# A windowed-attention and MLP block: one norm in halves, a copy on another engine, two transfers moved, the last inverses and copies in halves

## The chip, the cores and the metric

The kernel runs on one core of one Trainium2 chip. Times are device microseconds of one execution. A core has TensorE (PE in the profile; its weight loads are the row PEld), VectorE (DVE), ScalarE (ACT), GpSimd (POOL) and SyncE (SP), each of which runs its own instructions in order, and 16 DMA engines. Matmul results land in PSUM, eight banks of 128 x 512 fp32; everything else lives in SBUF or in DRAM.

## The reference

The input x has 2048 rows of 512. It is normalised, and the normalised rows go through an attention in which each row looks at eight earlier rows, two apart, and through a gelu block with a second norm; the first result, times the silu of the second, is added to x.

```python
def _A_ref(x, wqkv, wo):
    ...
    H = 32; Dh = D // H
    W, dil = 8, 2
    ...
    logits = jnp.einsum("bhsd,bhswd->bhsw", q, kg) * scale
    logits = jnp.where(mask[None, None, :, :], logits, -1e9)
    attn = _softmax(logits, axis=-1)
    o = jnp.einsum("bhsw,bhswd->bhsd", attn, vg)
    return (lambda x, *d: x.transpose(*d))(o, 0, 2, 1, 3).reshape(B, S, D) @ wo

def _B_ref(x, w1, w2, w3, w4):
    ...
    h = _gelu(_layernorm(x, axis=-1) @ w1)
    ...
    x1 = x + hs
    h2 = _gelu(_layernorm(x1, axis=-1) @ w3) @ w4
    return x1 + h2

x = A_x
xn = _layernorm(x, axis=-1)
s = _A_ref(xn, A_wqkv, A_wo)
g = _silu(_B_ref(xn, B_w1, B_w2, B_w3, B_w4))
return x + s * g
```

## The kernel before

Since the attention steps two rows at a time, the rows are split by parity p into two sets of 1024. Each set is two chunks of 512 rows (chunk c has p = c // 2), and a chunk is four tiles of 128 rows. The order of the instructions is written out by hand: every call below is pinned, and each engine and each DMA queue takes its instructions in the order of the program. Nearly all DMAs go through SP's queue.

**Opening.** `Norm` (line 213) holds one chunk's norm: `stats` (two VectorE instructions a tile, lines 224 and 226), `root` (line 235, two POOL instructions through `rsqrt_eps`, lines 207 and 208), `apply` (line 240, VectorE, a tile at a time, in place on `xn`). Chunk 0 is transposed on TensorE. For the other chunks `turn_dma` (line 322) issues one DMA transpose a tile on SP, into `xnT`. Lines 540 to 547 do the norm of chunk 1, with `scaled(0)` (line 293, a VectorE product that needs the row factors of chunk 0) between its statistics. `v_pair(0, 4)` and `v_pair(0, 6)` (lines 562 and 563) multiply tiles 0, 1 and then 2, 3 of chunk 1 by the v weights (line 371); `v_keep` (line 382) copies the result on ScalarE, and a DMA writes it to DRAM.

**Projections.** `proj` (line 332) writes two banks, a pair; `pair()` hands out three pairs in turn, so a projection waits until the pair three calls back has been read. `k_all` (line 358) copies each pair of k twice, times a 0/1 mask `em` of the even or the odd heads, into `kM` with stride 2: four ScalarE copies a chunk (line 363). `q_all`, `w1`, `w2` and `w3` follow the same way.

**Attention.** It runs in 18 units n, nine a parity. In unit n TensorE does the scores (line 639), the values and the sums of the weights of an earlier unit (`values`, lines 665 and 675), a share of the last MLP product (`g_w4`, line 777), and a final tile (`g_fin`, line 824). ScalarE does the exponential (line 646) and copies values (line 680), VectorE applies the mask (`band`, line 651). The sums are collected in batches of up to four units: `inverse` (line 687) takes a reciprocal on VectorE, `write_rec` (line 696) writes it to DRAM, `read_rec` (line 699) reads it back spread over the partitions, into four slots of `rr_t` (in the tile `ring`), and `apply` (line 712) multiplies the values by it. For the batches before the last full one the read comes as two halves of two slots, in two units. Batch 3 (units 12 to 15) has its inverses read in one piece at n = 17 (line 900) and applied in one piece after the loop (line 961). The last two units go through TensorE and ScalarE instead (`expand`, `keep_ps`, `apply_kept`, line 732).

**Final tiles.** `g_fin(p, i)` multiplies 128 rows of the attention by wo (four matmuls), copies the PSUM bank on ScalarE into `sg` (line 834), and does two VectorE products: times the gate in `xn` (line 838), plus x in `xo` (line 844, called `xo<-sg,xo`). The x is loaded again from DRAM by `load_xo` (line 491), two tiles a time, in the units that `xo_at` names; `stores` collects the writes of the result, two tiles each, and `flush_stores(n)` issues those that were noted in unit n or before. Each unit ends with its `load_xo` and `flush_stores(n - 2)` (lines 952 to 955). After the loop, lines 973 to 980 do tiles 1 to 6 of p = 1 whole, and tile 7 as two groups of 256 columns, each with its own copy, products and store, one on SP's queue and one on ScalarE's.

Of the kernel before, what the change touches and what calls it, by code (L numbers as in the profile page):

```python
# [8 lines left out]
AF = mybir.ActivationFunctionType  # L9
ALU = mybir.AluOpType  # L10
BF16 = mybir.dt.bfloat16
# [9 lines left out]
def kernel(  # L21
# [17 lines left out]
    PE, DVE, ACT, POOL, SP = nc.tensor, nc.vector, nc.scalar, nc.gpsimd, nc.sync  # L39

    def pin(ins):

        return tc.keep_in_program_order(ins)

    P = 128
    S = 2048
    D = 512
    F = 1376
    ND = D // P
# [4 lines left out]
    CH = 512  # L54
    NCH = S // CH
    TPC = CH // P
# [5 lines left out]
    NU = 2 * UP  # L62
# [6 lines left out]
    ov = out.flatten_outer_dims().rearrange("(m two) d -> two m d", two=2)  # L69
# [8 lines left out]
    fin = ctx.enter_context(tc.tile_pool(name="fin", bufs=8))  # L78
# [3 lines left out]
    def b8(shape, name):  # L82
        return big.tile(shape, BF16, name=name, tag="b8")
# [4 lines left out]
    PS = psp.tile([P, 8, CH], F32, name="PS")  # L88
# [12 lines left out]
    xn = [b8([P, M // P, D], f"xn{p}") for p in range(2)]  # L101
# [14 lines left out]
    for h in range(2):  # L116
        pin(SP.dma_start(
            out=wqk_sb[:, :, h * D // 2 : (h + 1) * D // 2], in_=wqkv_v[:, :, h * D // 2 : (h + 1) * D // 2]
# [31 lines left out]
    em = const.tile([P, 2], F32, name="em")  # L150
# [49 lines left out]
    kM = [kbp.tile([P, ND, MK, 2], BF16, name=f"kM{p}", tag="kM") for p in range(2)]  # L200
# [5 lines left out]
    def rsqrt_eps(dst, var):  # L206
        pin(POOL.tensor_scalar(out=dst, in0=var, scalar1=EPS, scalar2=None, op0=ALU.add))
        pin(POOL.tensor_tensor(out=dst, in0=dst, in1=nhalf[:, 0 : dst.shape[-1]], op=ALU.pow))
# [4 lines left out]
    class Norm:  # L213
# [18 lines left out]
            if half != 0:  # L232
                pin(DVE.reciprocal(out=r, in_=r))

        def root(self):
            rsqrt_eps(self.rstd, self.mv[:, :, 1])

        def apply(self, lo, hi):
            for j in range(lo, hi):
                pin(DVE.tensor_scalar(  # L240
                    out=self.dst[:, j, :], in0=self.src[:, j, :], scalar1=self.mv[:, j, 0:1],
                    scalar2=self.rstd[:, j : j + 1], op0=ALU.subtract, op1=ALU.mult,
                ))
# [46 lines left out]
    def scaled(c):  # L290
        p, k = c // 2, c % 2
        t = xn2Ts[c]
        pin(DVE.tensor_tensor(  # L293
            out=t, in0=xnT[p][:, :, k * CH : (k + 1) * CH],
            in1=t[:, ND - 1, :].unsqueeze(1).to_broadcast([P, ND, CH]), op=ALU.mult,
        ))
# [21 lines left out]
    def turn_dma(c, lo=0, hi=TPC):  # L318
        p, k = c // 2, c % 2
        for t in range(lo, hi):  # L320
            i = k * TPC + t
            pin(SP.dma_start_transpose(out=xnT[p][:, :, i * P : (i + 1) * P], in_=xn[p][:, i, :]))
# [20 lines left out]
    def chunk(t, c):  # L343
        p, k = c // 2, c % 2
        return t[p][:, :, k * CH : (k + 1) * CH]
# [9 lines left out]
        pin(POOL.memset(kM[p][:, :, 0:8, :], 0.0))  # L355
        pin(POOL.memset(kM[p][:, :, M + 8 : MK, :], 0.0))

    def k_all(c, parts=(0, 1)):
        p, k = c // 2, c % 2
        for a in parts:  # L360
            pt = proj(c, a, wqk_sb[:, :, D : 2 * D], chunk(xnT, c))
            for e in range(2):
                pin(ACT.activation(  # L363
                    kM[p][:, 2 * a : 2 * a + 2, 8 + k * CH : 8 + (k + 1) * CH, e], pt, AF.Copy, scale=em[:, e : e + 1]
                ))

    vn = {"n": 0}

# [117 lines left out]
    xo = {}  # L486
# [52 lines left out]
        q_keep(0, a, pq[a])  # L539
    l1 = Norm(x_of(1), x_of(1), TPC, "l1")  # L540
    l1.stats(0, 2)
    scaled(0)
    l1.stats(2, 4)
    l1.root()
    l1.apply(0, 4)
    turn_dma(1)
    rows2(1, l1)
    vputs = []
    k_all(0, (0,))
# [29 lines left out]
    while vputs:  # L579
# [4 lines left out]
    w1(1, 1)  # L584
    scaled(2)
    q_all(2)
    k_all(2)
    scaled(3)
    pin(SP.dma_start(
        out=w4_sb[:, 0 : NF - 1, :],  # L590
        in_=B_w4[0 : (NF - 1) * P, :].rearrange("(ft q) n -> q ft n", q=P),
# [106 lines left out]
    def read_rec(b, j=0, w=4):  # L698
        pin(SP.dma_start(
            out=rr_t[:, j : j + w].rearrange("p j a q -> p (j a q)"),  # L700
            in_=ap_of(rec_ds[b][:], [[16 * NQ, 16], [0, 8], [1, 4 * w * NQ]], 4 * j * NQ),
        ))
# [44 lines left out]
    free = [6, 7]  # L747
# [67 lines left out]
    stores = []  # L815
    now = {"n": 0}

    def g_fin(p, i, st=None, n=2, half=False, act=True, cols=None, later=None):

        c = slice(0, D) if cols is None else slice(*cols)  # L820
        W = c.stop - c.start

        def one(pt, dt):
            pin(PE.matmul(  # L824
                pt[:, 0:W], lhsT=oT[p][:, dt, i * P : (i + 1) * P], rhs=wo["sb"][:, dt, c],
                start=(dt == 0), stop=(dt == ND - 1),
            ))

        def done(pt):
            sg = fin.tile([P, D], BF16, name="sg", tag="f")[:, 0:W]  # L830
            pt = pt[:, 0:W]
            g = xn[p][:, i, c]
            if act:
                pin(ACT.activation(sg, pt, AF.Copy, scale=2.0 if half else 1.0))  # L834

            def steps():
                if act:
                    pin(DVE.tensor_tensor(out=sg, in0=sg, in1=g, op=ALU.mult))  # L838
                elif half:
                    pin(DVE.scalar_tensor_tensor(out=sg, in0=pt, scalar=2.0, in1=g, op0=ALU.mult, op1=ALU.mult))  # L840
                else:
                    pin(DVE.tensor_tensor(out=sg, in0=pt, in1=g, op=ALU.mult))
                x_o = xo[p][:, i, c]
                pin(DVE.tensor_tensor(out=x_o, in0=sg, in1=x_o, op=ALU.add))  # L844
                if cols is not None:
                    pin(st.dma_start(out=ov[p, i * P : (i + 1) * P, c], in_=x_o))
                elif st is not None:
                    stores.append((now["n"], lambda: store(st, p, i + 1 - n, n)))

            if later is None:  # L850
                steps()
            else:
                later.append(steps)

        return Group(ND, one, done)

    finals = []
    w4s = [g_w4(t, 2 if t == 15 else int(t > 12)) for t in range(16)]
# [7 lines left out]
    def flush(q):  # L866
        while q:
            q.pop(0)()

    def flush_stores(n):  # L870
        while stores and stores[0][0] <= n:
            stores.pop(0)[1]()
# [12 lines left out]
    HEAD, LAST = 6, 8  # L885
    W4 = 16 * NF - LAST - HEAD
    given = 0
    xo_at = {9: (1, 0), 12: (1, 2), 13: (1, 4), 15: (1, 6)}
    ends = {5: 0, 9: 1, 13: 2, 16: 3}
    load_va(0)  # L890
    for n in range(NU):
        now["n"] = n
        q = W4 * (n + 1) // NU - given
        given += q
        extra = small_g.get(n, [])
        if n == 0:
            w4_take(HEAD)

        if n == NU - 1:
            read_rec(3)  # L900
        for j in range(2):
            if n - 1 - j in ends and n < NU - 1:
                read_rec(ends[n - 1 - j], 2 * j, 2)
        if n == 15:
            values(13)
        scores(n)
        if 1 <= n < 16:
            band(n - 1)
        if n >= 2 and n != 15:
            values(n - 2 if n < 16 else n - 1)  # L910
        if n + 1 < NU:
            load_va(n + 1)
        if n == 4:
            load_wo()
        if n != 16:
            flush(finals)
        if n in ends:
            recs[ends[n]] = inverse()
            write_rec(ends[n])
        if n == 17:  # L920
            free += [2, 3]
            pin(ACT.preload_act_table_set("silu_and_others"))
        w4_take(q // 3)
        late = list(gates)
        gates.clear()
        flush(tanhs)
        if n == 15:
            apply(2, 0, 2)
        if n == 17:
            band(n)  # L930
        w4_take(q // 3, extra)
        if n < 15:
            flush(late)
        if 15 <= n < 17:
            band(n)
        if n == 16:
            flush(finals)
        if n == 15:
            values(14)
        w4_take(q - 2 * (q // 3), extra)  # L940
        for j in range(2):
            if n < 15 and n - 2 - j in ends:
                apply(ends[n - 2 - j], 2 * j, 2)
        if n == 16:
            apply(2, 2, 2)
        if n >= 15:
            flush(late)
            flush(gates)
        while extra:
            extra.pop(0).all()  # L950

        flush(vstores)
        if n in xo_at:
            load_xo(*xo_at[n])
        flush_stores(n - 2)

    n = NU
    now["n"] = n
    values(NU - 1)
    rec = inverse()  # L960
    apply(3)
    flush(gates)
    flush(tanhs)
    w4_take(LAST)
# [5 lines left out]
    flush(finals)  # L970
    for j in range(2):
        apply_kept(NU - 2 + j, kept[j])
    for i in range(1, 7):
        g_fin(1, i, SP if i % 2 or i == 6 else None, 1 if i == 6 else 2, half=i >= 5).all()
        if i != 6:
            flush_stores(n)
    g_fin(1, 7, SP, half=True, cols=(0, D // 2), later=finals).all()
    g_fin(1, 7, ACT, half=True, cols=(D // 2, D), later=finals).all()
    flush_stores(n)
    flush(finals)  # L980


# [28 lines left out]
```

## Time and profile before

| | |
|---|---|
| median of 3 runs | 195.97 us (195.82 to 197.27) |
| the profiled execution | 195.77 us |
| its span, first to last instruction | 194.0 us |
| mean granted TensorE clock | 0.997 |
| bytes read and written in DRAM | 17.14 MB and 6.59 MB |

The span is what the profile's rows cover; some 1.8 us of the execution lie around it. The page gives for each engine its busy time, and for each group of instructions the time its engine sat idle before it and what ended the wait. A line of the timeline reads: start, length, engine, line of the kernel, operation, output and input tiles with their shapes, number of instructions, and in brackets the idle time before the first of them with its releaser. Rows of the waits read: who waited, for whom, total time, number of waits, longest. "issue" is a wait for nothing that the profile shows. A few per cent of the matmul records can be missing.

Durations that the working uses, from the groups of instructions by form:

| work | mean or usual duration |
|---|---|
| statistics of a tile, two instructions on VectorE | 0.64 + 0.15 to 0.18 us |
| root on POOL, 128x4 | 0.23 + 1.04 us |
| apply of the norm, a tile | 0.41 us, 0.35 in a row |
| k copy on ScalarE, 128x1024 from PSUM, stride 2 | 1.40 us |
| DMA transpose, issue on SP | 1.22 us, the first 2.04 us |
| product with the inverses, 128x912 and 128x1824 | 0.62 and 1.11 us |
| copy of a final tile on ScalarE, 512 and 256 columns | 0.60 and 0.38 us |
| a final tile's two products on VectorE | 0.42 + 0.42 us |

### The profile page before, as it was taken

Reading aid. Unit: us, or ns where it says so; the run is one execution under the profiler, and the core shown is the slowest. Engines: PE = TensorE matmul, PEld = TensorE weight load, DVE = VectorE, ACT = ScalarE, POOL = GpSimd, SP = SyncE. Lnnn points to the kernel's source line nnn. Section 1 sums busy time; section 2 is a strip of 40 time slices with the busy share of each in tenths; the row PEclk is TensorE's granted clock in tenths of the full one; section 3 lists DMA queues with packets and bytes.
Section 4 is the critical chain, followed back from the end, with each engine's and each line's share of the span. In section 5 each row is a group of like instructions: output and inputs, shape, how many; then the busy total and the mean of one; then the engine's idle time right before and its main releaser. Section 6 shows DMA issues by size and latency. Waiting matters only on the chain.

```text
span 194.0 us, 5211 instructions
## 1 busy us (share of the span) xinstructions
PE 182.5 (94%) x2203; PEld 88.9 (46%) x2232; DVE 112.8 (58%) x226; ACT 132.7 (68%) x150; POOL 18.3 (9%) x58
## 2 busy tenths in 40 slices
PE   7999799999999999999999999999999999979990
PEld 2564344444444444444444444544454454544450
DVE  5896745220562996665000045565579789779694
ACT  7399838979258245165656787887778878876861
POOL 3006651000020022042000000000000000000000
PEclk9999999999999999999999999999999999999998
DMA  5999486479803113514700145356653753760724
GB/s 141 337 354 280 83 151 123 103 236 316 282 5 81 31 28 61 108 27 83 230 17 0 38 133 157 110 184 215 199 174 79 231 181 85 214 207 12 208 78 140
DMA packets 39859, 27.74 MB, mean 143 GB/s; under 512 B 18068, under 2 KB 39196, under 8 KB 39836
## 3 DMA queue, kind: packets, MB, share of 16 engines
q1 hardware_dynamic: 39692, 27.34, 50.4%
q8 instruction: 17, 0.28, 0.6%
q10 hardware_dynamic: 144, 0.07, 0.1%
q14 instruction: 6, 0.05, 0.1%
HBM read 17.14 MB, written 6.59 MB: 122 GB/s over the span
## 4 chain that ended last, share of the span: by engine, by line
PE 74%; ACT 9%; DVE 7%; DMA 5%; issue 3%; SPq 1%; ACTq 0%
PE PS L476 20%; PE PS L777 17%; PE PS L337 13%; ACT kM L363 8%; PE PS L436 5%; PE PS L808 4%; PE PS L824 3%; PE PS L665 3%; PE PS L639 3%; PE PS L371 3%; DMA ring<-rec_d 2%; DMA xn<-in_A_x_dram 2%; DVE xo L844 2%; DVE sg L838 2%; PE PS L675 2%
## 5 line engine op out<-in xcount | busy, mean ns | idle before, releaser
L476 PE MATMUL PS<-x1nT,w_sb 128*128 128x512 bf16 (+1 forms) x173 | 38.2, 379 | 0.2
L646 ACT ACTIVATE prob<-PS 128x1824 bf16<-128x1824 f32 x18 | 30.4, 1688 | 4.5 <-PE PS L639 3.7
L777 PE MATMUL PS<-w_sb,h3a 128*128 128x512 bf16 x112 | 29.3, 379 | 1.9 <-issue 1.7
L482 ACT ACTIVATE h3a<-PS 128x1024 bf16<-128x1024 f32 x16 | 16.4, 1024 | 20.6 <-PE PS L476 19.4
L790 DVE TENSOR_TENSOR xn<-PS,xn 128x512 bf16<-128x512 f32 x15 | 10.3, 685 | 31.8 <-PE PS L777 31.5
L476 PEld LDWEIGHTS <-w_sb 128*128 128x128 bf16 (+1 forms) x176 | 17.6, 100 | 20.4
L337 PE MATMUL PS<-xnT,wqk_sb 128*128 128x512 bf16 x110 | 24.9, 379 | 0.2
L363 ACT ACTIVATE kM<-PS,em 128x1024 bf16<-128x1024 f32 x16 | 20.8, 1401 | 2.2 <-PE PS L337 2.1
L651 DVE TENSOR_TENSOR prob<-prob,maskb 128x1824 bf16<-128x1824 bf16 x18 | 19.8, 1102 | 1.3 <-ACT prob L646 1.3
L777 PEld LDWEIGHTS <-h3a 128*128 128x128 bf16 x128 | 11.3, 97 | 13.4 <-issue 1.2
L444 DVE TENSOR_TENSOR xn<-PS,xn 128x1024 bf16<-128x1024 f32 x8 | 9.6, 1213 | 13.4 <-PE PS L436 13.4
L337 PEld LDWEIGHTS <-wqk_sb 128*128 128x128 bf16 x112 | 10.9, 97 | 13.3 <-issue 0.3
L824 PE MATMUL PS<-wo_sb,oT 128*128 128x512 bf16 (+1 forms) x68 | 15.6, 366 | 0.1
L834 ACT ACTIVATE sg<-PS 128x512 bf16<-128x512 f32 (+1 forms) x17 | 9.6, 572 | 7.4 <-PE PS L824 7.2
L337 PE MATMUL PS<-xn2T,w_sb 128*128 128x512 bf16 x62 | 14.4, 379 | 0.3 <-ACT kM L363 0.3
L436 PE MATMUL PS<-w_sb,hT 128*128 128x512 bf16 x63 | 14.4, 379 | 0.1
L382 ACT ACTIVATE vst<-PS 128x512 bf16<-128x512 f32 (+1 forms) x12 | 8.8, 736 | 7.5 <-DMA v_d<-vst 3.5
L777 PE MATMUL PS<-w_sb,h3b 128*128 128x512 bf16 (+1 forms) x44 | 12.8, 380 | 0.8 <-issue 0.8
L293 DVE TENSOR_TENSOR xn2T<-xnT,xn2T 128x2048 bf16<-128x2048 bf16 x4 | 4.9, 1217 | 11.8 <-DMA xn2T<-r_d 8.7
L409 ACT ACTIVATE hT<-PS 128x1024 bf16<-128x1024 f32 x8 | 7.9, 1038 | 4.3 <-PE PS L337 4.3
L224 DVE BATCH_NORM_STATS2 l1s<-xn 128x6 f32<-128x512 bf16 x16 | 10.1, 680 | 1.0 <-DMA xn<-in_A_x_dram 0.9
L224 DVE BATCH_NORM_STATS2 l3s<-xn 128x6 f32<-128x512 bf16 x16 | 10.3, 683 | 0.2
(104 smaller groups left out, 220.0 us busy)
## 6 DMA issues: line engine op xcount, KB each, us to landing
ring<-v_d SPq DMA_DIRECT2D x18, 256.0 KB, 2.7
v_d<-vst SPq DMA_DIRECT2D x16, 256.0 KB, 3.3
xo<-in_A_x_dram SPq DMA_DIRECT2D x8, 256.0 KB, 4.7
out_dram<-xo SPq DMA_DIRECT2D x7, 256.0 KB, 2.1
xn<-in_A_x_dram SPq DMA_DIRECT2D x6, 256.0 KB, 4.5
w_sb<-in_B_w_dram SPq DMA_DIRECT2D x1, 1376.0 KB
ring<-rec_d SPq DMA_DIRECT2D x6, 228.0 KB
w_sb<-in_B_w_dram SPq DMA_DIRECT2D x1, 1280.0 KB
```

The source lines that it names most:

```text
L224: pin(DVE.bn_stats(out=self.st[:, j, :], in_=self.src[:, j, :]))
L337: pin(PE.matmul(pt[:, b, :], lhsT=w[:, dt, nt * P : (nt + 1) * P], rhs=rhs[:, dt, :], start=(dt == 0), stop=(dt == ND - 1),))
L363: pin(ACT.activation(kM[p][:, 2 * a : 2 * a + 2, 8 + k * CH : 8 + (k + 1) * CH, e], pt, AF.Copy, scale=em[:, e : e + 1]))
L436: pin(PE.matmul(pt[:, j, :], lhsT=w2_src(p, g, m0), rhs=w2_sb[:, g, :], start=(g == 0), stop=(g == ND - 1),))
L444: pin(DVE.tensor_tensor(out=xs, in0=pts[h], in1=xs, op=ALU.add))
L476: pin(PE.matmul(pt[:fs, ft % 2, :], lhsT=w3_sb[:, dt, ft * P : ft * P + fs], rhs=x1nT[:, dt, :], start=(dt == 0), stop=(dt == ND - 1),))
L482: pin(ACT.activation(t[:, o : o + 2, :], pt, AF.Gelu_apprx_tanh))
L646: pin(ACT.activation(pr, S_ps[:, :, 0 : ND * NQ], AF.Exp, scale=SCALE))
L651: pin(DVE.tensor_tensor(out=f, in0=f, in1=maskb[:], op=ALU.min))
L777: pin(PE.matmul(pt, lhsT=h3_of(c, ft)[:fs, jj * P : (jj + 1) * P], rhs=w4_sb[:fs, ft, :], start=(ft == 0), stop=(ft == NF - 1 and silu < 2),))
L790: pin(DVE.tensor_tensor(out=x_i, in0=pt, in1=x_i, op=ALU.add))
L824: pin(PE.matmul(pt[:, 0:W], lhsT=oT[p][:, dt, i * P : (i + 1) * P], rhs=wo["sb"][:, dt, c], start=(dt == 0), stop=(dt == ND - 1),))
```

## The change

1. The norm of chunk 1: the root is taken for tiles 0 and 1 right after their statistics, and the two are applied and sent to their transposes before the statistics of tile 3; tiles 2 and 3 follow with a root of their own. `root` takes a range.
2. `k_all(2)` is called in two parts, with `scaled(3)` between them; in the second part the copy for the odd heads is done by VectorE from the same PSUM pair.
3. The last load of x, (1, 6), moves from the end of unit 15 to the end of unit 16, and unit 15 issues no stores; unit 16 issues what unit 15 would have.
4. The inverses of batch 3 are read in two DMAs of two slots each, both at n = 17, and applied in two products after the loop.
5. `g_fin` loses its arguments for columns and for work without ScalarE. With `parts=2` its matmuls run over the columns in two halves, the second half in another bank of the free list, with a ScalarE copy for each half into one tile `sg`; the two VectorE products and the store are whole. After the loop tiles 4 to 7 run so, tiles 1 to 3 as before; tile 7 has one store, on SP's queue.

```diff
-        def root(self):
-            rsqrt_eps(self.rstd, self.mv[:, :, 1])
+        def root(self, lo=0, hi=TPC):
+            rsqrt_eps(self.rstd[:, lo:hi], self.mv[:, lo:hi, 1])
...
-    def k_all(c, parts=(0, 1)):
+    def k_all(c, parts=(0, 1), both=True):
...
             for e in range(2):
...
+                dst = kM[p][:, 2 * a : 2 * a + 2, 8 + k * CH : 8 + (k + 1) * CH, e]
+                if e == 0 or both:
+                    pin(ACT.activation(dst, pt, AF.Copy, scale=em[:, e : e + 1]))
+                else:
+                    pin(DVE.tensor_scalar(out=dst, in0=pt, scalar1=em[:, e : e + 1], scalar2=None, op0=ALU.mult))
...
     l1.stats(0, 2)
+    l1.root(0, 2)
     scaled(0)
-    l1.stats(2, 4)
-    l1.root()
-    l1.apply(0, 4)
-    turn_dma(1)
+    l1.stats(2, 3)
+    l1.apply(0, 2)
+    turn_dma(1, 0, 2)
+    l1.stats(3, 4)
+    l1.root(2, 4)
+    l1.apply(2, 4)
+    turn_dma(1, 2, 4)
     rows2(1, l1)
...
-    k_all(2)
+    k_all(2, (0,))
     scaled(3)
+    k_all(2, (1,), both=False)
...
+    def g_fin(p, i, st=None, n=2, half=False, later=None, parts=1):
+
+        W = D // parts
+        sg = {}
+
+        def one(pt, k):
+            h, dt = k // ND, k % ND
+            c = slice(h * W, (h + 1) * W)
+            if dt == 0:
+                sg["no"] = free.pop(0) if h else None
+            if h:
+                pt = PS[:, sg["no"], :]
             pin(PE.matmul(
                 pt[:, 0:W], lhsT=oT[p][:, dt, i * P : (i + 1) * P], rhs=wo["sb"][:, dt, c],
                 start=(dt == 0), stop=(dt == ND - 1),
             ))
+            if dt == ND - 1:
+                if h == 0:
+                    sg["t"] = fin.tile([P, D], BF16, name="sg", tag="f")
+                pin(ACT.activation(sg["t"][:, c], pt[:, 0:W], AF.Copy, scale=2.0 if half else 1.0))
+                if h:
+                    free.append(sg["no"])
...
-    xo_at = {9: (1, 0), 12: (1, 2), 13: (1, 4), 15: (1, 6)}
+    xo_at = {9: (1, 0), 12: (1, 2), 13: (1, 4), 16: (1, 6)}
...
-        if n == NU - 1:
-            read_rec(3)
         for j in range(2):
-            if n - 1 - j in ends and n < NU - 1:
+            if n == NU - 1:
+                read_rec(3, 2 * j, 2)
+            elif n - 1 - j in ends:
                 read_rec(ends[n - 1 - j], 2 * j, 2)
...
-        flush_stores(n - 2)
+        if n != 15:
+            flush_stores(n - 2)
...
-    apply(3)
+    for j in (0, 2):
+        apply(3, j, 2)
...
-    for i in range(1, 7):
-        g_fin(1, i, SP if i % 2 or i == 6 else None, 1 if i == 6 else 2, half=i >= 5).all()
-        if i != 6:
-            flush_stores(n)
-    g_fin(1, 7, SP, half=True, cols=(0, D // 2), later=finals).all()
-    g_fin(1, 7, ACT, half=True, cols=(D // 2, D), later=finals).all()
-    flush_stores(n)
-    flush(finals)
+    for i in range(1, 8):
+        g_fin(1, i, (SP if i % 2 or i == 6 else None), 1 if i >= 6 else 2, half=i >= 5, parts=1 if i < 4 else 2).all()
+        flush_stores(n)
```

More of the change, by code (lines that the diff above doesn't have):

```diff
@@ L362, in k_all @@
             for e in range(2):
-                pin(ACT.activation(
-                    kM[p][:, 2 * a : 2 * a + 2, 8 + k * CH : 8 + (k + 1) * CH, e], pt, AF.Copy, scale=em[:, e : e + 1]
-                ))
+                dst = kM[p][:, 2 * a : 2 * a + 2, 8 + k * CH : 8 + (k + 1) * CH, e]
[3 more added lines that the diff above has]
+                    pin(DVE.tensor_scalar(out=dst, in0=pt, scalar1=em[:, e : e + 1], scalar2=None, op0=ALU.mult))
     vn = {"n": 0}
@@ L816 @@
     now = {"n": 0}
[L818 to L823, printed above, removed]
+    def g_fin(p, i, st=None, n=2, half=False, later=None, parts=1):
[8 more added lines that the diff above has]
+                pt = PS[:, sg["no"], :]
             pin(PE.matmul(
@@ L827, in one @@
             ))
-        def done(pt):
[L830 to L834, printed above, removed]
-            def steps():
[L837 to L847, printed above, removed]
+            if dt == ND - 1:
[4 more added lines that the diff above has]
+                    free.append(sg["no"])
+        def done(pt):
+            t = sg.pop("t")
+            def steps():
+                pin(DVE.tensor_tensor(out=t, in0=t, in1=xn[p][:, i, :], op=ALU.mult))
+                x_o = xo[p][:, i, :]
+                pin(DVE.tensor_tensor(out=x_o, in0=t, in1=x_o, op=ALU.add))
+                if st is not None:
                     stores.append((now["n"], lambda: store(st, p, i + 1 - n, n)))
@@ L853, in done @@
                 later.append(steps)
-        return Group(ND, one, done)
+        return Group(ND * parts, one, done)
     finals = []
```

## The prediction

> **What bounds the kernel now.** I read the page first, for the engine that fills the span.
>
> ```profile
> span 194.0 us, 5211 instructions
> PE 182.5 (94%) x2203; PEld 88.9 (46%) x2232; DVE 112.8 (58%) x226; ACT 132.7 (68%) x150; POOL 18.3 (9%) x58
> PE   7999799999999999999999999999999999979990
> PE 74%; ACT 9%; DVE 7%; DMA 5%; issue 3%; SPq 1%; ACTq 0%
> ```
>
> TensorE is full in nearly every slice. A change can pay where its digit drops (the first slice, the fifth at 19 to 24 us, the 36th at 170 to 175 us) and after its last matmul, at the end. So next came the list of waits, and in it TensorE's two rows.
>
> ```profile
> PEld L371 <- DMA xnT<-xn: 1.6, 1, 1.6
> ...
> PE PS L371 <- ACT vst L382: 1.1, 1, 1.1
> ...
> PE PS L665 <- issue: 0.8, 1, 0.8
> ...
> PEld L824 <- DVE oT L712: 0.6, 1, 0.6
> ```
>
> After the warm-up these are three holes, which the timeline places. The first:
>
> ```profile
> 17.09 6.16 SPq L322 DMA_TRANSPOSE xnT<-xn  x4
> 24.12 1.90 PE L371 MATMUL PS<-wv_sb,xnT 128*128 128x512 bf16 x7 [1.13 <-ACT vst L382]
> ```
>
> The matmuls put it down to ScalarE, their weight loads to the transposes. I believe the weight loads: the pair of banks that v_pair(0, 6) writes was freed by a gelu that ended at about 21.4 us, while the transposes' packets run until about 23.9 us. The second hole and the end:
>
> ```profile
> 172.84 0.27 PE L665 MATMUL PS<-prob,ring 128*32 128x57 bf16 x11 [0.78 <-issue]
> 178.19 0.57 SPq L699 DMA_DIRECT2D ring<-rec_d  x1
> 182.96 1.11 DVE L712 TENSOR_TENSOR oT<-oT,ring 128x1824 bf16<-128x1824 bf16 x1 [1.35 <-DMA ring<-rec_d]
> 182.98 6.50 PE L824 MATMUL PS<-wo_sb,oT 128*128 128x512 bf16 x32
> 184.12 5.09 PEld L824 LDWEIGHTS <-oT 128*128 128x128 bf16 x28 [0.61 <-DVE oT L712]
> 191.00 0.29 DVE L844 TENSOR_TENSOR xo<-sg,xo 128x256 bf16<-128x256 bf16 x1
> 191.32 0.37 ACTq L846 DMA_DIRECT2D out_dram<-xo  x1
> ```
>
> In the middle of values(14), TensorE waits 0.78 us for nothing the profile names. At the end VectorE sits idle until the inverses land (182.93), then works without a gap to 191.29; TensorE ends at 189.48. There VectorE sets the end, with TensorE close behind.
>
> **First norm in halves.** Before: the four statistics end at 15.17, POOL's root takes 15.26 to 16.61 (0.23 + 1.04 and gaps), the first apply ends at 17.06, and SP issues four transposes from 17.09 to 23.25. After, with the same rows: statistics of two tiles end at 12.65; POOL, idle for 12.8 us before, has their root ready at 14.1, under scaled(0) on VectorE (to 13.76). One more statistic (0.64 + 0.17) ends at 14.5, the first apply at 14.9, so SP starts 2.1 us earlier. The last two tiles have their root at about 17.5 and are applied by 18.25; SP comes to them at about 18.2 (2.04 + 1.22 for the first two), so it waits little, and ends at 20.8 instead of 23.25. The fourth lands 2.2 us after its issue starts, as now (21.85 to 24.11): 21.8, and TensorE asks at 22.6 to 23.0. The hole closes: **1.13 us**. Added: a second root on POOL (1.3 us, beside VectorE's work), and VectorE's next statistics 0.25 us later, covered by 0.75 us of idle time before their apply. Behind the transposes SP does the row factors' write, two v stores and the read of the factors; all come about 2 us earlier, so the v store that ScalarE waits for (27.5) does too. What is late next: from 24 us TensorE has no wait over 0.3 us up to 172 us, so the gain passes through.
>
> Against it stands the load queue. The DMA engines are full (share 1.1, 360 to 380 GB/s) until about 18.2 us; the first transpose's packets start at 18.36, and its issue took 2.04 us instead of 1.22. If the extra 0.8 us is the first transpose's own, the sum above holds. If SP is held until the loads are out, the first issue again ends at 19.13, and only about 0.2 us is won. The Trainium skill (DMA: Bandwidth & Descriptors, HWDGE ordering) says that each DMA engine consumes its descriptors in ring order; the trace agrees, with packets from 18.36 on, after the loads. By that rule alone, four times 1.0 us of packets from 18.3 end at 22.3, still before 22.6. I take 1.13, with 0.2 as the other end.
>
> **One k copy on VectorE.** ScalarE's last of four copies (1.40 us) goes. VectorE's nearest row is the 128x1024 sum from PSUM, 1.21 us. Nothing is queued behind it that is wanted before 50.7, since VectorE idles 7.5 us after scaled(3). scaled(3) itself is not later: it ran at 41.99, before the second pair of k is ready (43.5). w1(3, 0) waits for that pair. If VectorE reads beside ScalarE, the pair is free at 45.6; if after it, at 46.8, against 46.98 now. TensorE's wait there is at most 0.29. I count **0**; ends: 0.3 gained, or 1.0 lost if the strided write doubled the copy (48.0).
>
> **Late x and stores at n = 16.** A load (0.46 us of SP) and a store (0.46 us) of 256 KB each leave the queue at 167.92 and 168.43 and go in behind write_rec(3), at 175.7, ahead of read_rec(3). They leave a stretch with DMA share 0.92 to 1.07 (168 to 172.5). In it lies a 16 KB instruction transfer (170.48, 0.94 us long) and, after it, the 0.78 us hole, whose first instruction is the middle of a row of equal matmuls: I read it as instructions that came late through a full queue. With half the megabyte gone I take **0.70 us** won; ends 0 and 0.78. The next instruction transfers were at 174.4 and 183.2, outside the new place of the load and store (packets from about 177.0, 1.5 us at the 355 GB/s that such transfers reached at 168). SP's next work, read_rec(3), cannot start before the write has landed, at 177.3, so SP's two issues are hidden there. The x is wanted at 188.
>
> **Last inverses in halves.** Before, one read of 456 KB waits for the write (177.3) and then 0.9 us for the apply of slots 2 and 3 (178.17). After, the first half needs slots 0 and 1 only, free since 169.8: issue 177.3, packets from 178.6 behind the moved transfers, landed near 180.5; the second half is issued at 178.19 and lands by 182.3 (before, at 182.93). VectorE does the first apply at 181.65, right after the reciprocal (181.61), 0.62 us long, and the second by 182.9 instead of 184.07. The 0.3 us that TensorE loses at 184 goes. Next late: the kept factors of the last two units, from ScalarE at 184.27, so VectorE is done with them at 184.7, and seven tiles at 0.79 us (two products of 0.42, overlapped) end at **190.25**.
>
> **Column halves.** TensorE's last seven tiles run from 182.98 at 0.86 us each to 189.0. Tiles 4 to 7 are evicted in two copies of 0.38 instead of one of 0.60; 0.76 a tile stays under TensorE's 0.86, and the four banks of the free list come round only after two tiles (1.7 us), so no matmul waits for a bank. After the last matmul: 0.06 + 0.38 + 0.84 of VectorE gives **190.3**. Both limits agree, 0.95 before the present 191.29; the single last store (2.1 us to land) replaces two halves on two queues. I take **0.95**, ends 0.4 and 1.2.
>
> **The sum.** 1.13 + 0.70 + 0.95 = 2.8 us off the profiled execution's span of 194.0, which took 195.77 (1.77 lie around the span). That run is 0.20 under the median of three, 195.97. So 193.2 against that median.
>
> **Rivals.**
> *Transposes stay behind the loads.* For: the long first issue ending with its packets. Against: plain loads were issued in 0.5 us into a longer backlog at 13. Gain 0.2 + 0.7 + 0.95: 194.1. Chance 0.20.
> *The hole in values(14) stays, or moves to another boundary.* For: the trace names no cause, and the transfer had ended at 171.4. Against: it is the only one, and in the fullest stretch. 195.97 - 2.1: 193.9. Chance 0.23. The Trainium skill (Runtime: NRT & Kernel Launch, Instruction fetch mechanics) calls fetching mostly hidden; by it this case holds. Both of these together: 195.0, chance 0.08.
> *The tail gives only 0.4,* because the second half lands at 182.93 as before and VectorE's chain starts no earlier: 193.7. Chance 0.08.
> *Slower: the moved 512 KB hold up the late read.* VectorE's end is the second half's landing plus 7.6 us (now 8.4). Beyond 183.7 the tail loses, and beyond 185.5 it eats the other two gains. At 170 GB/s, this read's own rate before, the 968 KB land at 183.3; at the span's mean of 122 GB/s at 185.6, which is 196.1; at 83 GB/s, the slowest full slice of the opening, at 189.3, some 199.8. Against: 355 GB/s in rows of this kind. Chance 0.07.
>
> **How the numbers follow.** The forecast has 0.34. One per cent, 1.96 us, is about what a measurement can tell from no change: under 194.0 is faster. The forecast, half of the cases near 193.9 and 194.1, and most of the tail case make 0.60; slower by over 1% is most of the last rival (from about 100 GB/s down), 0.05; the rest 0.35. The range takes the k copy's 0.3 and the tail's 1.2 below, and both first rivals together above: 192.5 to 195.1. The forecast alone is 192.6 to 193.7.
>
> **What would show it.** Right: v_pair(0, 6) follows v_pair(0, 4) without a gap, and the first transpose is issued near 15; no wait in values(14); the first apply of the last inverses right after the reciprocal at the end, the second under 0.7 us later; VectorE's last product 1.3 us after the last matmul. Wrong: a first transpose issue of 4 us; a wait on DMA before the second apply; TensorE waiting on VectorE's k copy.

## The result and the profile after

The changed kernel took 194.49 us in the median (194.01 to 194.60), beside 196.12 us for the kernel before (195.82 to 197.27): a ratio of 0.9905, 95% interval 0.9878 to 0.9933. In a later series the same kernel gave 0.9949 (0.9921 to 0.9978). So it is faster by 0.5 to 1%. The forecast was 193.2 us (range 192.5 to 195.1), a gain of 2.8 us; the medians give 1.6. The profiled execution has a span of 192.6 us, 1.4 us less than that of before.

The page's head first: TensorE's digit is 9 in the fifth slice now, and the 36th went from 7 to 8.

```profile
span 192.6 us, 5267 instructions
PE 185.7 (96%) x2244; PEld 90.2 (47%) x2244; DVE 114.5 (59%) x226; ACT 132.2 (69%) x152; POOL 20.4 (11%) x60
PE   7999999999999999999999999999999999989990
PE 75%; ACT 8%; DMA 6%; DVE 6%; issue 1%; SPq 1%
```

The waits of the matmuls and of the weight loads come next. The hole on the transposes and the wait on the apply of the inverses are gone. The wait in values(14) is there, smaller, and one on VectorE's k copy stands where one on ScalarE's (0.29 us) was.

```profile
PE PS L673 <- issue: 0.5, 1, 0.5
PE PS L337 <- DVE kM L368: 0.2, 1, 0.2
```

The timeline of the opening shows the transposes from 15.65 on, where they were from 17.09, and sixteen matmuls of the two v pairs in a row.

```profile
15.65 5.65 SPq L322 DMA_TRANSPOSE xnT<-xn  x4
21.61 3.62 PE L374 MATMUL PS<-wv_sb,xnT 128*128 128x512 bf16 x16
```

The timeline of the end, on SP's queue and VectorE:

```profile
173.08 1.30 SPq L704 DMA_DIRECT2D rec_d<-rec  x2
174.43 0.45 SPq L494 DMA_DIRECT2D xo<-in_A_x_dram  x1
174.92 0.47 SPq L749 DMA_DIRECT2D out_dram<-xo  x1
...
176.52 1.24 SPq L707 DMA_DIRECT2D ring<-rec_d  x2
...
179.55 0.87 DVE L695 RECIPROCAL rec<-PS 128x114 bf16<-128x114 f32 x1 [0.56 <-PE PS L683]
181.52 1.31 DVE L720 TENSOR_TENSOR oT<-oT,ring 128x912 bf16<-128x912 bf16 x2 [1.10 <-DMA ring<-rec_d]
```

VectorE still waits 1.10 us for the first half of the inverses (1.35 before for the whole). The first half was issued 3.4 us after the write was, and landed 5.0 us after that.

To place the 1.4 us I cut both spans at four TensorE weight loads that both programs have: A, the 35th, a transpose of chunk 0 between the first q matmuls; B, the second of v_pair(0, 6); C, the second of w1(3, 0); D, the fourth in `expand`, at the end. The times come from the traces; the second profile is of a later execution of the same kernel.

| us | start to A | A to B | B to C | C to D | D to the end | span |
|---|---|---|---|---|---|---|
| before | 8.79 | 15.34 | 22.91 | 135.65 | 11.28 | 194.0 |
| after | 9.31 | 14.03 | 23.04 | 135.11 | 11.10 | 192.6 |
| after, second profile | 9.31 | 13.82 | 23.05 | 136.11 | 10.65 | 192.9 |

Before A the two programs do the same work, so the 0.52 us lost there is the opening's scatter: over all kernels of this study A lay between 8.74 and 10.25 us. The halved norm won 1.3 us (A to B), the k copy cost 0.13 (B to C), and the end won 0.2 in one profile and 0.6 in the other. C to D holds the wait in values(14), which was 0.53 us in one execution of this kernel and 1.36 in another: that stretch scatters too.

### The profile page after: what moved, and what is told of

The parts are those of the page before. It is cut to its first block, busy times and chain, and to the rows that moved or that the text cites. A ratio compares the mean times of both kernels' runs of the same rounds, so it can differ in the third digit from the quotient of the medians.

```text
span 192.6 us, 5267 instructions
## 1 busy us (share of the span) xinstructions
PE 185.7 (96%) x2244; PEld 90.2 (47%) x2244; DVE 114.5 (59%) x226; ACT 132.2 (69%) x152; POOL 20.4 (11%) x60
## 4 chain that ended last, share of the span: by engine, by line
PE 75%; ACT 8%; DMA 6%; DVE 6%; issue 1%; SPq 1%
PE PS L479 20%; PE PS L785 18%; PE PS L337 14%; ACT kM L366 7%; PE PS L439 5%; PE PS L816 4%; PE PS L838 3%; PE PS L673 3%; PE PS L647 3%; PE PS L374 3%; DMA ring<-rec_d 3%; DMA xn<-in_A_x_dram 2%; PE PS L683 2%; DVE sg L853 2%; DMA rec_d<-rec 1%
## 5 line engine op out<-in xcount | busy, mean ns | idle before, releaser
L785 PE MATMUL PS<-w_sb,h3a 128*128 128x512 bf16 x128 | 32.7, 380 | 0.0
L366 ACT ACTIVATE kM<-PS,em 128x1024 bf16<-128x1024 f32 x15 | 19.5, 1400 | 2.2 <-PE PS L337 2.1
L845 ACT ACTIVATE sg<-PS 128x512 bf16<-128x512 f32 (+1 forms) x20 | 10.1, 512 | 6.2 <-PE PS L838 5.9
L785 PE MATMUL PS<-w_sb,h3b 128*128 128x512 bf16 (+1 forms) x48 | 13.5, 381 | 0.0
L838 PEld LDWEIGHTS <-oT 128*128 128x128 bf16 x80 | 7.8, 98 | 6.2 <-issue 0.3
```

Source lines behind the costliest of these rows:

```text
L366: pin(ACT.activation(dst, pt, AF.Copy, scale=em[:, e : e + 1]))
L785: pin(PE.matmul(pt, lhsT=h3_of(c, ft)[:fs, jj * P : (jj + 1) * P], rhs=w4_sb[:fs, ft, :], start=(ft == 0), stop=(ft == NF - 1 and silu < 2),))
L838: pin(PE.matmul(pt[:, 0:W], lhsT=oT[p][:, dt, i * P : (i + 1) * P], rhs=wo["sb"][:, dt, c], start=(dt == 0), stop=(dt == ND - 1),))
L845: pin(ACT.activation(sg["t"][:, c], pt[:, 0:W], AF.Copy, scale=2.0 if half else 1.0))
```

## The experiments

Since the opening and one wait scatter by more than most effects here, each kernel is read by these stretches first and by its time second. The stretch most used is from the end of the last reciprocal on VectorE to the end of the span, "the tail": 12.36 us before, 12.17 after. Each of these is one execution. Two more kernels below have the old end, the front alone (12.11) and the one with fewer warm-up matmuls (12.04): against those the changed kernel won nothing at the end in its first profile.

**The front alone**

```diff
 # the kernel before, with only (root takes a range, as in the change):
     l1.stats(0, 2)
+    l1.root(0, 2)
     scaled(0)
-    l1.stats(2, 4)
-    l1.root()
-    l1.apply(0, 4)
-    turn_dma(1)
+    l1.stats(2, 3)
+    l1.apply(0, 2)
+    turn_dma(1, 0, 2)
...
```

> The kernel before with the norm of chunk 1 in halves and nothing else. Theory (the four transposes alone held v_pair(0, 6)): no wait between the two v pairs, the weight loads of the second follow at once; everything after comes 1.1 to 1.3 us earlier, to the end: about 195.0 us, ratio 0.994. The hole in values(14) stays at 0.8 us and the read of the last inverses still takes 4.7 us from its issue. Rival (the gain is lost again before 171 us, since TensorE then waits for something that was hidden): the hole at 23 us is gone, but the ratio is over 0.998.

Measured: 194.64 us, ratio 0.9935 (0.9907 to 0.9963). A to B took 14.03 us, 1.31 less than before, with no wait between the v pairs; B to C stayed at 22.90, C to D at 135.5. The gain passes through to the end, and alone it is about as large as the whole change's. Its size scatters with the hole that it closes: the kernel with fewer warm-up matmuls has the old front, and there the hole was 0.7 us and A to B 14.91. In this profile the wait in values(14) was 0.5 us with the load and the store where they had always been, which the change had been forecast to mend.

**The late load put back**

```diff
-    xo_at = {9: (1, 0), 12: (1, 2), 13: (1, 4), 16: (1, 6)}
+    xo_at = {9: (1, 0), 12: (1, 2), 13: (1, 4), 15: (1, 6)}
...
-        if n != 15:
-            flush_stores(n - 2)
+        flush_stores(n - 2)
```

> The changed kernel with the last load of x and the stores back at the end of unit 15. Theory A (the 512 KB put ahead of the two halves of the last inverses delayed them): the halves land 3.5 to 4.2 us after their issue instead of 5.0, VectorE's first apply follows the reciprocal within 0.4 us (1.1 now); the hole in values(14) is 0.8 us again instead of 0.53; in sum 0.1 to 0.5 us under the changed kernel, about 194.2. Theory B (a half read takes its 5 us whatever lies ahead of it): the wait of 1.1 us stays, and only the hole grows: about 194.8.

Measured: 194.73 us, ratio 0.9920 (0.9884 to 0.9956), span 191.5; tail 11.74 us. The timeline of this kernel's VectorE and of its SP queue:

```profile
172.40 1.30 SPq L704 DMA_DIRECT2D rec_d<-rec  x2
175.12 1.76 SPq L707 DMA_DIRECT2D ring<-rec_d  x2
...
178.86 0.87 DVE L695 RECIPROCAL rec<-PS 128x114 bf16<-128x114 f32 x1 [0.57 <-PE PS L683]
179.65 1.11 DVE L720 TENSOR_TENSOR oT<-oT,ring 128x912 bf16<-128x912 bf16 x2
...
181.97 0.84 DVE L740 TENSOR_TENSOR oT<-oT,rk 128x456 bf16<-128x456 bf16 x2 [0.42 <-ACT rk L734]
```

The applies follow the reciprocal at once, and theory A holds. The semaphores in the traces tell when each DMA landed. The first half landed 2.92 us after its issue here and 4.98 us in the changed kernel, where the packets of the moved load and store run from 176.2 to 178.6 and those of the first half begin at 178.1. The write counts too, for less: its second part landed 2.00 us after its own issue here and 2.71 in the changed kernel, where the load and the store are queued behind it, so the first half is issued 2.7 us after the write instead of 3.4. The second profile of the changed kernel lies between: 4.45, 2.51 and 3.25 us. The other half of theory A fell: the wait in values(14) did not grow back to 0.8, it was 0.2 us.

**The late load behind the reads**

```diff
-    xo_at = {9: (1, 0), 12: (1, 2), 13: (1, 4), 16: (1, 6)}
+    xo_at = {9: (1, 0), 12: (1, 2), 13: (1, 4), 17: (1, 6)}
...
-        if n != 15:
+        if n not in (15, 16):
             flush_stores(n - 2)
```

> The changed kernel with the last load of x and the held-back stores in unit 17, behind the two reads of the last inverses. Theory A: the halves land early as in the run before, and the hole in values(14) stays at 0.53, so both gains hold: about 193.9. Theory B: the landing stays at 5.0 us after the issue, time as the changed kernel, 194.5.

Measured: 193.43 us, ratio 0.9883 (0.9827 to 0.9940; four runs only); tail 11.74, no wait for the inverses, first half issued 2.75 us after the write and landed 2.99 us later; the wait in values(14) 0.3 us. Theory A: the place ahead of the reads was what cost the tail. Whether the load is far ahead or behind makes no difference to the tail (11.74 both times). In all eight kernels with the halved read and the load elsewhere the first half landed 2.9 to 3.1 us after its issue, 1.4 to 1.7 us before the reciprocal ended.

**Two products ahead of the applies**

```diff
 # on the kernel with the late load behind the reads
+    flush(finals)
     for j in (0, 2):
         apply(3, j, 2)
     flush(gates)
```

> As the run before, and the two products of the final tile (1, 0) are put ahead of the applies of the last inverses on VectorE. Theory A (VectorE sets the end, and has 0.8 us of work that does not need the inverses): its last product comes 0.3 to 0.6 us earlier, TensorE's matmuls then end at most 1.4 us before it: about 193.5. Theory B (the read is late): the products fill the 1.1 us wait and the end comes 0.5 us earlier than in the changed kernel: 194.0. If neither moves the time, the end is set by TensorE and not by VectorE.

Measured: 193.92 us, ratio 0.9925 (0.9894 to 0.9957); tail 11.72 instead of 11.74. Neither theory: once the inverses are in time, VectorE waits for the kept factors from ScalarE (0.42 us in the fence above and here), and the last product ends 1.34 us after the last matmul with or without the two products moved. The end is TensorE's then. The span was 193.2, since A lay at 10.25: TensorE waited 0.9 us for the first weights.

**Whole final tiles, and one read**

```diff
 # whole_tiles: g_fin and the last loop of the kernel before
 # one_read:
-                read_rec(3, 2 * j, 2)
+            read_rec(3)
...
-    for j in (0, 2):
-        apply(3, j, 2)
+    apply(3)
```

Both stand on the kernel with the load behind the reads.

> The kernel with the late load behind the two reads (the run behind_read), and the final tiles copied as before: tiles 1 to 6 whole, tile 7 as two groups of 256 columns with two stores. From the end of the last reciprocal on VectorE to the end of the span it was 11.8 us there (12.4 in the kernel before, 12.2 in the changed one). Theory (the column halves take VectorE's last products from 1.8 us behind the last matmul to 1.3): 12.1 to 12.3, the last matmul still 7.6 us after the reciprocal. Rival (the earlier inverses are the whole gain of the tail): 11.8.

> The kernel with the late load behind the reads, and the last inverses read in one piece and applied in one piece as before. Theory (the halves let the first read start 1 us before the apply that frees slots 2 and 3, and let VectorE start on the first half): VectorE waits 0.8 to 1.4 us for the read again, and from the last reciprocal to the end 12.0 to 12.2 us. Rival (without the moved load ahead of it the one read lands in time too): 11.8 us and no wait.

Measured, one execution each (194.31 and 193.78 us): with whole tiles the tail is 11.93, with one read 11.82, with both halvings 11.74. So the column halves are worth 0.2 us: VectorE's last product comes 1.34 us after the last matmul instead of 1.74, but from there to the end pass 2.79 us instead of 2.61. One store of 128 KB replaces two of 64 KB on two queues there; over all kernels that stretch took 2.76 to 2.87 us with the one and 2.61 to 2.68 with the two. The halved read is worth nothing that shows beside the column halves. VectorE does wait 0.75 us for the one read, which landed 4.1 us after its issue, but its last product still comes 1.34 us after the last matmul; the 0.08 us lie behind that product.

**The k copy on ScalarE, and spread**

```diff
 # k_on_act
-    k_all(2, (0,))
-    scaled(3)
-    k_all(2, (1,), both=False)
+    k_all(2)
+    scaled(3)
 # k_spread
-    k_all(2, (0,))
     scaled(3)
+    k_all(2, (0,), both=False)
     k_all(2, (1,), both=False)
```

> The kernel with the late load behind the reads, and all four k copies of chunk 2 on ScalarE again. Theory (VectorE's copy starts only when ScalarE's is done and is 0.1 us longer than what it saves): TensorE waits 0.3 us before w1(3, 0) instead of 0.4, and all that follows comes 0.1 us earlier: 0.1 us under behind_read, which no timing will resolve. Rival (ScalarE, freed 1.3 us earlier, has time left for its gelus): TensorE's wait is over 0.6 us.

> The kernel with the late load behind the reads, and the copies for the odd heads of both pairs of chunk 2 on VectorE, behind scaled(3). Theory (the pairs of k come free one copy earlier when ScalarE and VectorE take turns on them): the second pair is free at 45.4 instead of 46.2, TensorE does not wait before w1(3, 0), and what follows comes 0.3 to 0.4 us earlier than in behind_read. Rival (scaled(3) or the order of the two reads of one pair holds VectorE): the wait is 0.4 us or more.

Measured, B to C: 22.91 us with all copies on ScalarE, 23.05 with one on VectorE, 22.67 with one of each pair on VectorE; the times, 194.00 us (0.9926, 0.9893 to 0.9959) and 194.13 (0.9920, 0.9889 to 0.9951), don't tell them apart. What both expectations say of TensorE's wait is met. The timeline of the spread kernel shows why:

```profile
40.49 1.41 ACT L366 ACTIVATE kM<-PS,em 128x1024 bf16<-128x1024 f32 x1 [0.70 <-PE PS L337]
41.94 1.36 DVE L368 TENSOR_SCALAR kM<-PS,em 128x1024 bf16<-128x1024 f32 x1 [0.40 <-ACT kM L366]
42.22 1.41 ACT L366 ACTIVATE kM<-PS,em 128x1024 bf16<-128x1024 f32 x1 [0.32 <-PE PS L337]
43.66 1.37 DVE L368 TENSOR_SCALAR kM<-PS,em 128x1024 bf16<-128x1024 f32 x1 [0.36 <-ACT kM L366]
```

VectorE's copy of a pair starts when ScalarE's of the same pair has ended, never beside it; the profile names that copy as what it waits for. Taking turns over two pairs, the engines overlap on different pairs; with VectorE on the last copy alone there is nothing to overlap, and its 1.36 us come after ScalarE's third, which in the changed kernel freed the pair 0.1 us later than ScalarE's fourth would have. The Trainium skill (PSUM — Partial Sum Buffer, PSUM bank collisions raise a hardware error) says that two engines must be kept off one bank at the same time, reads included; the order in this trace agrees, with VectorE 0.04 us after ScalarE.

**All chunks spread, and TensorE's instructions shifted**

```diff
 # k_spread_all: the apply of chunk 3's norm first, then
+    l3.apply(0, 4)
     q_all(1)
-    k_all(1)
-    l3.apply(0, 4)
+    k_all(1, both=False)
...
-    k_all(3)
+    k_all(3, both=False)
 # aligned: the same, and
-    for i in range(10):
+    for i in range(8):
         pin(PE.matmul(
             PS[:, 6 + i % 2, :], lhsT=ones_bf[:], rhs=ones_bf.unsqueeze(1).to_broadcast([P, TPC, P]),
             start=True, stop=True,
         ))
+    for i in range(84):
+        rg = i % 4
+        pin(PE.matmul(
+            PS[32 * rg : 32 * rg + 32, 6, 0:QB], lhsT=ones_bf[:, 0:32], rhs=ones_bf[:, 0:QB], start=True, stop=True,
+            tile_position=(0, 32 * rg),
+        ))
 # fewer_warm: the kernel before, and only
-    for i in range(10):
+    for i in range(8):
```

> As k_spread, and the copies for the odd heads of chunks 1 and 3 go to VectorE too (the apply of chunk 3's norm ahead of chunk 1's projections, so that VectorE's queue is not held). Theory (each chunk's last ScalarE copy holds TensorE for 0.2 to 0.3 us before the next projection, and VectorE idles there): another 0.2 us for each of the two chunks; v_pair(0, 6) to the last reciprocal 0.4 us shorter than in k_spread, about 0.988 of the kernel before. Rival (TensorE's small waits there have another cause): no further change against k_spread.

> As k_spread_all, with the ten warm-up matmuls replaced by eight and 84 small ones (32 rows of weights, 57 columns), 164 TensorE instructions more. Theory (the hole near 171 us is TensorE waiting for a block of 256 instructions that it crosses into there; it was seen at two places 254 instructions apart): the crossings move by 92 instructions, so there is no hole in the middle of values(14) or of the attention unit before it; what is left anywhere else is under 0.3 us. Rival (the hole belongs to the work at that place, a wait for va_r or the probabilities): it stays after the 21st matmul, at 0.2 to 0.8 us.

> The kernel before with eight warm-up matmuls instead of ten, that is four TensorE instructions fewer. Theory (a crossing into a new block of instructions): the hole in values(14) comes after 23 of the 32 matmuls instead of 21. Rival (a wait of that work): after 21, as before.

Measured: all chunks spread 193.80 us, 0.9924 (0.9894 to 0.9953); shifted 193.90, 0.9924 (0.9895 to 0.9953). Spreading chunk 3 does not pay: its second copy holds VectorE until 62.3 us, the sums and statistics of w2(1) slip, and TensorE waits in w3(0). Only the shifted kernel, which has the same copies, has that wait too (0.7 us). Chunk 1's spread shows as 0.1 us in B to C, 22.57 in both kernels instead of 22.67.

```profile
PE PS L479 <- DVE xn L447: 0.7, 1, 0.7
```

The wait in values(14) belongs to a place in TensorE's own stream of instructions and not to the work there. With four instructions fewer ahead of it (one execution, 194.88 us), it comes after 23 matmuls instead of 21:

```profile
171.20 0.36 PE L665 MATMUL PS<-prob,ring 128*32 128x57 bf16 x23
172.30 0.26 PE L665 MATMUL PS<-prob,ring 128*32 128x57 bf16 x9 [0.74 <-issue]
```

In the kernel with all chunks spread two such waits show, in the scores (0.38 us after the 19th matmul) and in values(14) (0.81), with 127 weight loads between them, so some 254 instructions. The other traces agree: wherever the rows of small matmuls stall in the second half of the span, it is behind the 1238th, the 1875th or the 2002nd recorded weight load, which are 5 times 127.4 and 127 apart. And with 164 instructions more in front, the row of 32 is whole:

```profile
170.29 0.40 PE L653 MATMUL PS<-qT,kM 32*128 32x57 bf16 x32
170.62 0.42 PE L679 MATMUL PS<-prob,ring 128*32 128x57 bf16 x32
170.87 0.38 PE L689 MATMUL PS<-prob,den_st 128*32 128x114 bf16 x16
```

That kernel has no wait for instructions over 0.2 us among its matmuls. Its timed median is no better than that of the one without the shift, so what the timing shows of it is nothing yet; in the two profiles C to D is 135.00 against 136.91, of which the two waits are 1.2.

**The changed kernel once more**

> The changed kernel once more. If the halves of the last inverses are late because of the 512 KB ahead of them, VectorE again waits about 1 us for them after the last reciprocal and 12.1 to 12.3 us pass from there to the end. If that was chance in one execution, the wait is gone and it is 11.8 us.

Measured: 194.75 us, ratio 0.9949 (0.9921 to 0.9978). The expectation is met by half: VectorE waits for the inverses again, but 0.4 us, and the tail is 11.72. The wait in values(14) was the longest of all:

```profile
172.44 0.27 PE L673 MATMUL PS<-prob,ring 128*32 128x57 bf16 x11 [1.36 <-issue]
181.59 1.22 DVE L720 TENSOR_TENSOR oT<-oT,ring 128x912 bf16<-128x912 bf16 x2 [0.38 <-DMA ring<-rec_d]
```

So with the load ahead of the reads VectorE waits 0.4 to 1.1 us (both profiles of this kernel); in the eight kernels with the halved read and the load elsewhere there was no such wait. What a wait costs can be read across the kernels. TensorE's last matmul ends 7.6 us after the reciprocal in every one of them but the kernel before (7.88). With a wait of 0.4 us (here) or 0.75 (one read), VectorE's last product still comes 1.34 us after it, as without a wait, when VectorE waits 0.4 us later on for the kept factors. In the four profiles with a wait of about 1 us or more (1.35, 1.09 and 0.98 with the old end, 1.10 in the changed kernel) the tail is 11.0 to 11.1 us plus the wait. So VectorE has some 0.7 us to spare, an estimate from these numbers, and only what goes beyond them lengthens the end.

## Why the prediction was right or wrong

The range held the time; the point was 1.3 us too low, by two terms. That the range held is in part luck: its upper end stands for the transposes behind the loads together with the hole in values(14) that stays. Only the second of these came, and the tail fell short in place of the first. The prediction's own terms for what did come, 1.13 and a tail of 0.4, give 194.4 us.

*The first norm in halves*, 1.13 us: right, 1.3 us in A to B, with the mechanism shown alone. The rival that SP is held until the loads are out fell: the first transposes were issued at 15.65 and 17.06 in 1.30 and 1.20 us, with the engines full of loads until about 18.6, and the third took 1.64. The long first issue of 2.04 us was chance, as far as one more profile tells: it was 1.31 in the kernel with fewer warm-up matmuls, whose front is the old one. The first two transposes did land late, at 21.1 and 21.6 us, 5.5 and 4.5 us after their issue; in the kernel before it was 20.3 and 21.7. What the prediction worked out from the ring order of the Trainium skill (DMA: Bandwidth & Descriptors, HWDGE ordering) came out: the last of the four landed at 22.5, where it had 22.3, and v_pair(0, 6) had no wait.

*One k copy on VectorE*, 0: nearly, a loss of 0.13. The strided copy took 1.36 us, not the 1.21 of the nearest row, and comes after ScalarE's, which was one of the two cases given.

*Late x and stores*, 0.70 won: wrong in its cause, and the rival that the hole stays came true. The wait is late instructions, as the prediction read it, but not because of that load and store: it was 0.5 us with them at their old place (the front alone), 0.2 (put back), 0.53 and 1.36 with them moved. By position it belongs to a crossing every 256 instructions or so, by length it scatters from one execution to the next. One profile of 0.78 us was taken for a fixed cost. The Trainium skill (Runtime: NRT & Kernel Launch, Instruction fetch mechanics) gives blocks of 256 instructions, with which the 254 counted here agree, and calls the fetch mostly hidden; here it was not, with waits of up to 1.4 us at up to three places of a kernel. That fetching a block is what TensorE waits for is the reading that fits; the runs show the place and the period, not the fetch.

*The last inverses in halves and the column halves*, 0.95: mis-sized, 0.2 and 0.6 in the two profiles. The step that failed is the first half's landing: "issue 177.3, packets from 178.6 behind the moved transfers, landed near 180.5", 3.2 us after its issue. It took 4.98 and 4.45 us with the moved transfers ahead of it, and 2.9 to 3.1 with them elsewhere. A smaller part is "SP's two issues are hidden there": they are, but with the two transfers queued behind it the small write of the sums landed 0.5 to 0.7 us later than in the kernel with the load put back, so the read was issued later too. The rival of a tail that gives only 0.4 came nearest; its reason, a second half that lands as late as the whole read did, held: the half landed 1.8 us after the reciprocal, the whole read had landed 1.3 us after it. With the load out of the way 0.6 us were won against the profile of the kernel before, 0.3 to 0.4 against the other two profiles of the old end, and 0.2 of it came from the column halves, by the one profile without them. The working of the tiles itself held there (last product 1.34 us after the last matmul, forecast 1.3), but TensorE ended 7.6 us after the reciprocal, not 7.4, and the single store cost 0.1 to 0.2.

*The slower rival* did not come; its mechanism, the moved 512 KB ahead of the late read, did, at a small price. The second half landed 1.8 us after the reciprocal, and by the prediction's figures the tail loses from 2.1 us on.

Two slips in the working change nothing: both first rivals together add up to 194.8 us, not 195.0, and the slice of 83 GB/s was not a full one, since the engines' digit there is 4.

What stays open: how much the end won beyond its scatter, with three profiles of the old end (12.04 to 12.36) and two of the changed one (11.72 and 12.17); and whether the spread copies of chunk 2 together with the shifted instructions, without those of chunk 3, beat the rest. That pair was not tried. The smallest ratio measured was that of the load behind the reads, 0.9883, with an interval that overlaps those of all the others.

## What to carry to other kernels

A wait that one profile shows for no reason of the program is to be looked for in a second profile before it is put into a sum; shifting the instructions by a few tells whether it belongs to the work or to the place in the stream. When a transfer is moved into a quiet stretch of a queue, ask what is issued behind it and when that must land, not only whether its issue is hidden: here the read behind it took 1.5 to 2 us longer to land, and the small write ahead of it 0.5 to 0.7. Then ask how much the engine that waits has to spare, since only the rest is lost. Work given to a second engine helped where the two took turns on different banks; on the same bank it came after.

## What the runs showed of the hardware that was not expected

- At one place in TensorE's stream of instructions, the middle of a row of small matmuls, its wait varied between nothing (the spread kernel) and 1.4 us (the second profile of the changed kernel) from one execution to the next, and no such wait was left in the kernel with 164 instructions more in front.
- A DRAM write of two times 28.5 KB landed 2.7 to 2.9 us after the issue of its first part with nothing queued behind it (twelve kernels), 3.2 and 3.4 us with a load and a store of 256 KB each behind it.
- The first read of 228 KB issued behind that load and store landed 4.4 to 5.0 us after its issue, and 2.9 to 3.1 us with them elsewhere.
- Transposes issued into full DMA engines held SP hardly longer than others: 1.20 and 1.30 us for the first two, 1.64 for the third (1.85 in the front alone), but the first of them landed 5.5 us after its issue.
